# A quarter of 21 products moved from VectorE to ScalarE and GpSimd, in an induced attention with a gated feed-forward layer

## The chip, the core and the metric

The kernel runs on one core of one Trainium2 chip. A core has five engines that run side by side and wait for each other by semaphores: TensorE (PE; its weight loads are shown as PEld), VectorE (DVE), ScalarE (ACT), GpSimd (POOL) and SyncE (SP, here a queue for DMAs). Each engine takes its own instructions strictly in the order in which the program gives them. Matmul results land in PSUM, which has 8 banks of 512 f32 columns; GpSimd cannot read PSUM, so what it is to work on must first be copied to SBUF. The metric is the time of one execution in microseconds of device time.

## The reference

An input of 4 batches of 12,416 rows of 128 channels goes through an induced set attention: 32 inducing vectors attend to the rows of a batch, and the rows attend to the result. What comes out, 49,664 rows, goes through a feed-forward layer with a sigmoid gate.

```
def mab(q, kv):
    s = scale * (q @ kv.transpose(0, 2, 1))
    s = s - s.max(-1, keepdims=True)
    a = np.exp(s)
    a /= a.sum(-1, keepdims=True) + 1e-09
    return a @ kv
h = mab(I, x)                 # I: the 32 inducing vectors, for each batch
y = mab(x, h)                 # 4 x 12416 x 128

gate = 1.0 / (1.0 + np.exp(-(y @ w_gate)))     # w_gate, w_val: 128 x 1536
val = y @ w_val
out = gate * val @ w_out                       # w_out: 1536 x 128
```

## The kernel before

The attention part is called stage 1 (inducing vectors over rows) and stage 2 (rows over the 32 vectors h). Stage 2 is never finished into y: the kernel folds h into the weights (`hw`, 32 rows in place of 128), so that both hidden matmuls of the feed-forward layer take the normalised attention weights `a2` (32 rows) as their input. Four such matmuls of 32 rows can be placed beside each other on TensorE; here the two of the value part and the two of the gate.

The feed-forward part is the frame of the whole program. Rows are taken in *blocks* of 512 (4 chunks of 128). The hidden width of 1536 is 12 slices of 128. For each block there are eight *steps*, alternately of two slices (`cnt=2`, 1024 columns) and of one (`cnt=1`, 512 columns). A pair of steps is called a slot here (one of 1024 and one of 512). Each batch has 24 blocks, 192 steps, 96 slots. For step t:

- `hidden_mm(st, "v")` fills the value's PSUM tile `v_ps` and, in `gate_fill(t + 2)`, the gate's `g_ps` of two steps later. The two-slice tiles have a double bank each (`v2`, `g2`), the one-slice tiles a bank each (`v1`, `g1`), and each tile exists once: v of step t can be filled only when the product of step t − 2 is done, g of step t + 2 only when the gate of step t is done. One bank (`acc`) gathers the output, one (`m`) serves stage 1 and 2.
- `gate(t)` on ScalarE writes t = tanh(g / 2) to SBUF as f16 (L1053).
- `product(t)` on VectorE makes u = (t + 1) · v, f16, in one instruction (L1071). The factor one half is applied at the very end.
- `project` issues the output matmuls (L1106), four per slice, with u as weights, one per chunk, and gathers 12 slices in `acc`. After a block's last slice ScalarE scales the bank into `o32` (L1124) and SyncE stores it.

In the main loop, step t issues `product(t)`, then `gate(t + 2)`, then what the plan puts beside this slot (all of stage 1 and 2 for later rows, cut in pieces by `plan_...` functions and hung on slots by number), and on odd steps `project` with room for 3 slices (4 when more than 3 are waiting). So the order on every engine is written out by this loop; no scheduler changes it. For products of two slices from step 4 on, the kernel replaces the wait for the gate by a hand-made one for the gate's fill of t + 2, which itself comes after the gate.

From the last third of the fourth batch on (`T0`) the gates are made ahead slice by slice, and all products are of two slices. A product of two slices there reads its gate from a ring in `xn`; this part is the same before and after.

Of the kernel before, what the change touches and what calls it, by code (L numbers as in the profile page):

```python
# [17 lines left out]
P = 128  # L18
GC = 16
BC = 4  # L20
# [6 lines left out]
def kernel(  # L27
# [90 lines left out]
    def keep_on(n, tag, src=idle):  # L118
        w_ps = ps.tile([P, 4, P], F32, tag=tag, name="w_ps")
        for _ in range(n):  # L120
            nc.tensor.matmul(w_ps[:], src[:, 0, :], src, start=True, stop=True)
# [11 lines left out]
        out=identf[:],  # L133
        in_=identf[:],
# [13 lines left out]
    wo16 = const.tile([P, NJ, C], F16, tag="wo16")  # L148
# [648 lines left out]
    for p in range(-2, NS - 3):  # L797
# [40 lines left out]
    c0, n = groups[sc]  # L838
# [3 lines left out]
    for j0, tag, copy in ((GC // 2, "v2", nc.scalar.copy), (GC - BC, "g1", nc.vector.tensor_copy)):  # L842
# [35 lines left out]
    for g in range(4):  # L878
# [4 lines left out]
            start=False,  # L883
            stop=True,
            skip_group_check=True,
# [12 lines left out]
        out=e32l[:], in0=e32[:], scalar1=lsum[:], scalar2=TINY, op0=ALU.mult, op1=ALU.add  # L898
# [16 lines left out]
    def h_add(k, first=False, last=False):  # L915
# [15 lines left out]
        out=nmx_a[:], in_=s2_a[:, 0:BC, :], axis=AX.X, op=ALU.max, negate=True  # L931
# [11 lines left out]
    for hf, tag in enumerate(("g1", "v1")):  # L943
# [41 lines left out]
    steps = []  # L985
    blocks = []
    first_step = {}
# [11 lines left out]
    T0 = first_step[(B - 1, 0)] + 2 * 16  # L999
    assert gates[T0]["j0"] == 0  # L1000
    steps = gates[:T0]
    singles = []
    for i in range(gates[T0]["block"], len(blocks)):
        for j in range(0, NJ, 2):
            steps.append(dict(block=i, j0=j, cnt=2, bank="vw" if j % 4 else "v2"))
        singles += [dict(block=i, j0=j, cnt=1, bank=f"gw{j % 3}") for j in range(NJ)]
    NST = len(steps)

    def hidden_mm(st, what, halves=False):
        tag = st.get("bank") or f"{what}{st['cnt']}"  # L1010
        pt = ps.tile([P, st["cnt"], 512], F32, tag=tag, name=f"{what}_ps")
        pieces, col = [], 0
        for b, c, nb in blocks[st["block"]]:
            pieces += [(k, b, c, nb, col) for k in range(st["cnt"])]
            col += nb * P
        if not halves and st["block"] < len(blocks) - 1:
            pieces.sort(key=lambda p: p[0])
        for k, b, c, nb, col in pieces:
            j = st["j0"] + k
            r = 32 * (j % 2 + (2 if what == "v" else 0))  # L1020
            a2r, o = a2[(b, c)]
            st[what + "end"] = nc.tensor.matmul(  # L1022
                pt[:, k, col : col + nb * P],
                hw[b][r : r + 32, j // 2, :],
                a2r[r : r + 32, o : o + nb, :].rearrange("p j t -> p (j t)"),
                start=True,
                stop=True,
            )
        st[what] = pt

    def gate_fill(t):
        if t < T0 + 2:
            hidden_mm(gates[t], "g", t == 0)

    def ring_t(i, n):
        c = i % 24 * BC
        return xn[B - 2][:, c : c + n * BC, :].rearrange("p (j a) c -> p j (a c)", a=BC)

    def single_fill(i):
        if i < len(singles):  # L1040
            hidden_mm(singles[i], "g")
# [5 lines left out]
    def gate(t):  # L1047
        if t < T0 + 2:
# [3 lines left out]
            for c, e in zip(cuts, cuts[1:]):  # L1052
                st["tanh"] = nc.scalar.activation(  # L1053
                    out=st["t"][:, :, c:e], in_=st["g"][:, :, c:e], func=AF.Tanh, scale=0.5
                )

    def product(t):
        st = steps[t]
        hidden_mm(st, "v")
        if t == 0:  # L1060
            keep_on(3, "acc")
        if t < T0:
            gate_fill(t + 2)
        else:
            single_fill(2 * (t - T0) + 3)
            single_fill(2 * (t - T0) + 4)
            st["t"] = ring_t(2 * (t - T0), 2)
        st["u"] = up.tile([P, st["cnt"], 512], F16, tag=f"u{st['cnt']}", name="u16")
        cuts = [0, 256, 512] if t == 0 else [0, 512] if t < NST - 1 else [0, 384, 512]
        for c, e in zip(cuts, cuts[1:]):  # L1070
            u = nc.vector.scalar_tensor_tensor(  # L1071
                out=st["u"][:, :, c:e],
                in0=st["t"][:, :, c:e],
                scalar=1.0,
                in1=st["v"][:, :, c:e],
                op0=ALU.add,
                op1=ALU.mult,
            )
# [12 lines left out]

    def project(upto, now, room):
        while queue and queue[-1][0] < upto and room > 0:
            t, k = queue.pop()
            st = steps[t]
            j = st["j0"] + k
            if j == 0:
                acc[0] = ps.tile([P, BC, C], F32, tag="acc", name="acc_ps")
            todo = [(k, i) for i in range(BC)]
            if t == NST - 1:  # L1100
                k, _ = queue.pop()[1], None
                j = st["j0"] + k
                todo = [(n, i) for n in range(2) for i in range(BC - 1)] + [(n, BC - 1) for n in range(2)]
            for n, i in todo:
                e = st["j0"] + n
                nc.tensor.matmul(  # L1106
                    acc[0][:, i, :],
                    st["u"][:, n, ts(i, P)],
                    wo16[:, NI * (e % 2) + e // 2, :],
                    start=(e == 0 and i == 0),  # L1110
                    stop=(e == NJ - 1),
                    skip_group_check=True,
                )
            room -= 1
            if t == NST - 1:
                o32 = op.tile([P, BC, C], F32, tag="o32")
                nc.scalar.mul(out=o32[:, 0:2], in_=acc[0][:, 0:2], mul=0.5)
# [3 lines left out]
            elif j == NJ - 1:  # L1121
                block = blocks[st["block"]]
                o32 = op.tile([P, BC, C], F32, tag="o32")
                nc.scalar.mul(out=o32[:], in_=acc[0][:], mul=0.5)  # L1124
# [8 lines left out]
    for b in range(B):  # L1133
# [6 lines left out]
        for s in range(3 if b == 0 else 2, NG - 1):  # L1140
            k = o + 16 * s - 28
# [76 lines left out]
    for t in range(T0):  # L1218
        product(t)
        gate(t + 2)  # L1220
        if t % 2 == 0:
            beside(t // 2, False)
        else:
            beside(t // 2, True)
            project(t - 1, t, 3 if waiting(t - 1) <= 3 else 4)
    narrow.close()
    ps.open(ctx, "psw", "vw", "gw0", "gw1", "gw2")
    for t in range(T0, NST):
        product(t)
        six, part = divmod(t - T0, 3)  # L1230
        single_gate(2 * (t - T0) + 3)
        for i in range(2):
            if not project(t - 1, t, 1) and waiting(t - 1) >= 2:
                project(t - 1, t, 1)
# [36 lines left out]
```

## Time and profile before

| | |
|---|---|
| median of 3 runs | 713.96 us (713.81 to 714.0) |
| span of the profiled execution | 712.4 us |
| VectorE busy | 694.2 us (97%) |
| ScalarE busy | 678.6 us (95%) |
| TensorE busy | 649.5 us (91%) |
| GpSimd busy | 449.2 us (63%) |
| granted TensorE clock, mean | 0.998 |

The span runs from the first to the last instruction of one profiled execution; the time of a run holds some 1.6 us more. In the lists, a row gives line, engine, operation, output and inputs, shapes and the number of instances, then the busy time in all and the mean of one in ns, and behind the second bar the idle time of the engine just before these instructions with what ended it. In the list by time a row is a run of like instructions on one engine: its start, how long it lasts from its first start to its last end, and their number. Instructions on an engine overlap a little: the next one starts before the last one's end, so a step from start to start is shorter than the duration.

### The profile page before, as it was taken

To read this page: it belongs to the slowest core of one execution; us is meant where nothing else is said; L and a number is where in the kernel's file an instruction comes from. 1 tells how busy PE (TensorE), PEld (TensorE's weight loads), DVE (VectorE), ACT (ScalarE), POOL (GpSimd) and SP (SyncE) were. 2 spreads that over 40 slices of the span, in tenths; PEclk is the share of its full clock that TensorE was granted. 3 is DMA by queue.
4 is the path that set the end of the run, shared out by engine and by line. 5 is a ranking of instruction groups with operands and counts; after the bars stand their busy time and mean duration, and the time that the engine had idled before them with its cause. 6 is when DMAs were issued, how large, how long until landed. Compare 5 with 4: busy or idle time off the path is not lost.

```text
span 712.4 us, 21620 instructions
## 1 busy us (share of the span) xinstructions
PE 649.5 (91%) x8475; PEld 394.2 (55%) x8475; DVE 694.2 (97%) x806; ACT 678.6 (95%) x1103; POOL 449.2 (63%) x785
## 2 busy tenths in 40 slices
PE   7999899998999999999998989999899999899996
PEld 4555455555555555655555655555555555555555
DVE  4799999999999999999999999999999999999997
ACT  4799999999999999999999999999999999999996
POOL 4568865877558978668657887587748356372300
PEclk9999999999999999999999999999999999999999
DMA  8979964263693174155485142221222131221201
GB/s 171 176 136 174 149 129 103 76 120 81 118 159 81 57 126 103 56 120 114 92 149 112 53 76 67 55 76 38 70 76 61 46 60 60 61 61 46 71 37 46
DMA packets 117110, 65.23 MB, mean 92 GB/s; under 512 B 100208, under 2 KB 101392, under 8 KB 117008
## 3 DMA queue, kind: packets, MB, share of 16 engines
q1 hardware_dynamic: 112320, 49.83, 31.4%
q0 software_dynamic: 4416, 13.90, 11.1%
q8 instruction: 66, 1.08, 0.6%
q14 instruction: 36, 0.29, 0.1%
q10 hardware_dynamic: 272, 0.13, 0.1%
HBM read 27.80 MB, written 25.43 MB: 75 GB/s over the span
## 4 chain that ended last, share of the span: by engine, by line
DVE 38%; PE 30%; issue 15%; ACT 14%; DMA 2%; DVEq 1%; POOL 0%; ACTq 0%; POOLq 0%
DVE u L1071 36%; PE acc_ps L1106 14%; PE v_ps L1022 11%; ACT t L1053 11%; PE g_ps L1022 2%; DMA xn<-in_x_dram 2%; ACT o L1124 2%; ACT xn L1045 1%; PE hp_ps L296 1%; DVE nm L248 1%; DVEq L1071 0%; POOL xn L95 0%; ACT a1T L261 0%; ACT e L662 0%; ACT hwt L483 0%
## 5 line engine op out<-in xcount | busy, mean ns | idle before, releaser
L1071 DVE SCALAR_TENSOR_TENSOR u<-t,v_ps 128x512 f16<-128x512 f16 x609 | 528.8, 947 | 1.0 <-ACT t L1053 0.5
L1053 ACT ACTIVATE t<-g_ps 128x512 f16<-128x512 f32 x609 | 464.5, 821 | 11.0 <-ACT t L1053 4.3
L1106 PE MATMUL acc_ps<-wo,u 128*128 128x128 f16 x4656 | 334.5, 220 | 3.2 <-ACT o L1124 0.8
L1106 PEld LDWEIGHTS <-u 128*128 128x128 f16 x4656 | 262.7, 98 | 112.9 <-issue 109.4
L1022 PE MATMUL v_ps<-a2r,hwt 32*128 32x512 f16 (+1 forms) x1188 | 278.6, 372 | 47.1 <-DVE u L1071 43.5
L1022 PE MATMUL g_ps<-a2r,hwt 32*128 32x512 f16 (+1 forms) x1188 | 293.6, 376 | 0.5 <-DVE u L1071 0.2
L1022 PEld LDWEIGHTS <-hwt 32*128 32x128 f16 x2424 | 92.0, 91 | 156.7 <-issue 104.3
L1071 DVE SCALAR_TENSOR_TENSOR u<-xn,v_ps 128x1024 f16<-128x1024 f16 (+1 forms) x127 | 142.9, 1206 | 0.3 <-PE g_ps L1022 0.3
L1045 ACT ACTIVATE xn<-g_ps 128x512 f16<-128x512 f32 x249 | 129.0, 606 | 1.9 <-PE g_ps L1022 0.6
L692 POOL TENSOR_TENSOR a2n<-e,rs 128x2048 f16<-128x2048 f16 (+3 forms) x25 | 86.8, 3475 | 5.0 <-DVE rs L681 2.1
L670 POOL TENSOR_TENSOR sum<-e 128x256 f32<-128x256 f16 (+1 forms) x23 | 15.4, 672 | 117.0 <-ACT e L662 117.0
L453 POOL TENSOR_TENSOR near<-sme,minus 128x16 f32<-128x16 f32 (+1 forms) x22 | 65.2, 2964 | 1.6
L1124 ACT ACTIVATE o<-acc_ps 128x512 f32<-128x512 f32 x96 | 58.0, 604 | 0.0
L647 POOL TENSOR_SCALAR rise<-rise 128x256 f32<-128x256 f32 (+6 forms) x110 | 30.3, 275 | 9.6
L650 POOL TENSOR_TENSOR top<-top,rise 128x128 f32<-128x128 f32 (+3 forms) x88 | 28.5, 323 | 7.3
L670 POOL TENSOR_TENSOR sum<-sum 128x128 f32<-128x128 f32 (+3 forms) x92 | 28.4, 309 | 7.2
L646 POOL TENSOR_TENSOR rise<-top 128x128 f32<-128x128 f32 (+3 forms) x88 | 27.3, 311 | 6.9
L646 POOL TENSOR_TENSOR rise<-sc 128x256 f32<-128x256 f32 (+1 forms) x18 | 13.3, 736 | 21.2 <-ACT sc L636 21.1
L653 POOL TENSOR_TENSOR sc<-sc,top 128x512 f32<-128x512 f32 (+1 forms) x18 | 19.5, 1086 | 1.4
L602 PEld LDWEIGHTS <-xT 128*128 128x128 f16 x388 | 13.1, 96 | 11.7 <-issue 11.3
L95 POOL DMA_DIRECT2D xn<-in_x_dram x25 | 15.0, 607 | 6.5 <-DMA xn<-in_x_dram 5.6
L602 PE MATMUL s_ps<-hT,xT 128*128 128x32 f16 x388 | 18.1, 178 | 0.1
(161 smaller groups left out, 321.7 us busy)
## 6 DMA issues: line engine op xcount, KB each, us to landing
out_dram<-o SPq DMA_DIRECT2D x96, 256.0 KB, 2.1
xn<-in_x_dram POOLq DMA_DIRECT2D x19, 512.0 KB, 7.2
xn<-in_x_dram POOLq DMA_DIRECT2D x4, 544.0 KB, 6.0
a2r<-a2n SPq DMA_TRANSPOSE x29, 4.4
xT<-xn SPq DMA_TRANSPOSE x27, 4.4
xn<-in_x_dram POOLq DMA_DIRECT2D x1, 384.0 KB, 14.9
wg<-in_moe_w_gate_dram POOLq DMA_DIRECT2D x1, 384.0 KB, 16.4
wv<-in_moe_w_val_dram POOLq DMA_DIRECT2D x1, 384.0 KB, 16.4
```

Source lines behind the costliest of these rows:

```text
L453: nc.gpsimd.tensor_tensor(out=near, in0=x, in1=minus, op=ALU.pow)
L602: nc.tensor.matmul(s2[:, j, :], xT[b][:, c + j, :], hT16[b][:], start=(j == 0), stop=whole and j == j1 - 1, skip_group_check=True,)
L646: nc.gpsimd.tensor_tensor(out=r, in0=far, in1=near, op=ALU.subtract)
L647: nc.gpsimd.tensor_scalar(out=r, in0=r, scalar1=BIG, scalar2=0.0, op0=ALU.min, op1=ALU.max)
L670: nc.gpsimd.tensor_tensor(out=d[:, 0:n, :], in0=src[:, :, 0:w], in1=src[:, :, w : 2 * w], op=ALU.add)
L692: eng.tensor_tensor(out=a2n[:, 0:n, :, :], in0=e.unsqueeze(2).to_broadcast((P, n, 4, m)), in1=rs.unsqueeze(2).unsqueeze(3).to_broadcast((P ...
L1022: st[what + "end"] = nc.tensor.matmul(pt[:, k, col : col + nb * P], hw[b][r : r + 32, j // 2, :], a2r[r : r + 32, o : o + nb, :].rearrange ...
L1045: nc.scalar.activation(out=ring_t(i, 1), in_=singles[i]["g"][:], func=AF.Tanh, scale=0.5)
L1053: st["tanh"] = nc.scalar.activation(out=st["t"][:, :, c:e], in_=st["g"][:, :, c:e], func=AF.Tanh, scale=0.5)
L1071: u = nc.vector.scalar_tensor_tensor(out=st["u"][:, :, c:e], in0=st["t"][:, :, c:e], scalar=1.0, in1=st["v"][:, :, c:e], op0=ALU.add, op1= ...
L1106: nc.tensor.matmul(acc[0][:, i, :], st["u"][:, n, ts(i, P)], wo16[:, NI * (e % 2) + e // 2, :], start=(e == 0 and i == 0), stop=(e == NJ - 1),
L1124: nc.scalar.mul(out=o32[:], in_=acc[0][:], mul=0.5)
```

## The change

In each of the first three batches seven slots (k = 5, 33, 49, 65, 77, 85, 93; in all of them the step of two slices is the block's second, slices 3 and 4) are put in the set `aside`. There:

- ScalarE copies the last 256 of the 1024 columns of `v_ps` to SBUF as f32 (`far`). The copy is issued behind the fill of v and ahead of `gate(t + 2)`.
- VectorE makes the first 768 columns of u in one instruction.
- GpSimd makes the last 256 columns in two: mid = far · t, u = mid + far.
- The output matmuls for these 256 columns (slice 4, chunks 2 and 3) go behind all others of their block.

The queue of output matmuls is now in single matmuls in place of slices, with room for 14 per call, and 9 just after an aside step. The buffers of u are 6 for two slices, as before, and 4 for one. For the products of steps t + 2, t + 4 and t + 6 behind an aside step t the hand-made wait is left out, so that they wait for fill and gate as the framework finds it.

```diff
+    aside = set()
+    for b in range(B - 1):
+        for k in (5, 33, 49, 65, 77, 85, 93):
+            aside.add(first_step[(b, 0)] + 2 * k)
+    after = {t + d for t in aside for d in (2, 4, 6)}
...
+    def aside_take(t):
+        st = steps[t]
+        st["far"] = tp.tile([P, 256], F32, tag="far", name="far", bufs=2)
+        nc.scalar.copy(out=st["far"], in_=st["v"][:, 1, 256:512])
+
+    def aside_product(t):
+        st = steps[t]
+        mid = tp.tile([P, 256], F32, tag="mid", name="mid", bufs=1)
+        nc.gpsimd.tensor_tensor(out=mid, in0=st["far"], in1=st["t"][:, 1, 256:512], op=ALU.mult)
+        nc.gpsimd.tensor_tensor(out=st["u"][:, 1, 256:512], in0=mid, in1=st["far"], op=ALU.add)
...
     def product(t):
         st = steps[t]
         hidden_mm(st, "v")
...
+        if t in aside:
+            aside_take(t)
-        st["u"] = up.tile([P, st["cnt"], 512], F16, tag=f"u{st['cnt']}", name="u16")
+        st["u"] = up.tile(
+            [P, st["cnt"], 512], F16, tag=f"u{st['cnt']}", name="u16", bufs=6 if st["cnt"] == 2 else 4
+        )
...
+        if t in aside:
+            nc.vector.scalar_tensor_tensor(
+                out=flat(st["u"][:])[:, 0:768],
+                in0=flat(st["t"][:])[:, 0:768],
+                scalar=1.0,
+                in1=flat(st["v"][:])[:, 0:768],
+                op0=ALU.add,
+                op1=ALU.mult,
+            )
+            aside_product(t)
+            return
...
-        if st["cnt"] == 2 and 4 <= t < T0:
+        if st["cnt"] == 2 and 4 <= t < T0 and t not in after:
...
-    queue = [(t, k) for t in range(NST) for k in range(steps[t]["cnt"])]
+    queue = [(t, k, i) for t in range(NST) for k in range(steps[t]["cnt"]) for i in range(BC)]
+    for t in aside:
+        end = max(k for k in range(NST) if steps[k]["block"] == steps[t]["block"])
+        for i in (2, 3):
+            queue.remove((t, 1, i))
+            queue.insert(queue.index((end, steps[end]["cnt"] - 1, BC - 1)) + 1, (t, 1, i))
...
-            project(t - 1, t, 3 if waiting(t - 1) <= 3 else 4)
+            project(t - 1, t, 9 if t - 1 in aside else 14)
```

How this stands on ScalarE around step 154 (k = 77 of the first batch). Before: gates (t), the output copy o of the block before, gates. In brackets are the semaphores that an instruction waits for, named by the engine that raises them.

```order
L1053 ACTIVATE t_3717<-g_ps 128x1024 [waits DVE_49,PE_49,Activation_49]
L1053 ACTIVATE t_3725<-g_ps 128x512 [waits DVE_49,PE_49]
L1124 ACTIVATE o_3739<-acc_ps 128x512 [waits DMAHW4_49,PE_49]
L1053 ACTIVATE t_3750<-g_ps 128x1024 [waits DVE_49,PE_49,Activation_49]
L1053 ACTIVATE t_3758<-g_ps 128x512 [waits DVE_49,PE_49]
```

And of the change, the same stretch:

```order
L1058 ACTIVATE t_3737<-g_ps 128x1024 [waits DVE_49,PE_49,Activation_49]
L1058 ACTIVATE t_3745<-g_ps 128x512 [waits DVE_49,PE_49]
L1160 ACTIVATE o_3759<-acc_ps 128x512 [waits DMAHW4_49,PE_49]
L1065 COPY far<-v_ps 128x256 [waits PE_49]
L1058 ACTIVATE t_3775<-g_ps 128x1024 [waits DVE_49,PE_49,Activation_49]
L1058 ACTIVATE t_3783<-g_ps 128x512 [waits DVE_49,PE_49]
```

The copy far stands between the output copy and the gate of step 156.

On VectorE the products around the same step were, the third of these being that of step 154:

```order
L1071 SCALAR_TENSOR_TENSOR u_3715<-t_3687,v_ps 128x1024 [waits DVE_49,PE_49]
L1071 SCALAR_TENSOR_TENSOR u_3723<-t_3695,v_ps 128x512 [waits PE_49,Activation_49]
L1071 SCALAR_TENSOR_TENSOR u_3748<-t_3717,v_ps 128x1024 [waits DVE_49,PE_49]
L1071 SCALAR_TENSOR_TENSOR u_3756<-t_3725,v_ps 128x512 [waits PE_49,Activation_49]
L1071 SCALAR_TENSOR_TENSOR u_3779<-t_3750,v_ps 128x1024 [waits DVE_49,PE_49]
L1071 SCALAR_TENSOR_TENSOR u_3787<-t_3758,v_ps 128x512 [waits PE_49,Activation_49]
```

and are now:

```order
L1105 SCALAR_TENSOR_TENSOR u_3735<-t_3707,v_ps 128x1024 [waits PE_49]
L1105 SCALAR_TENSOR_TENSOR u_3743<-t_3715,v_ps 128x512 [waits PE_49,Activation_49]
L1094 SCALAR_TENSOR_TENSOR u_3770<-t_3737,v_ps 128x768 [waits Activation_49]
L1105 SCALAR_TENSOR_TENSOR u_3781<-t_3745,v_ps 128x512 [waits PE_49]
L1105 SCALAR_TENSOR_TENSOR u_3801<-t_3775,v_ps 128x1024 [waits PE_49,Activation_49]
L1105 SCALAR_TENSOR_TENSOR u_3809<-t_3783,v_ps 128x512 [waits PE_49,Activation_49]
```

The product of step 154 is of 768 columns and waits for ScalarE where it waited for TensorE; that of step 156 waits for both.

On GpSimd the two new operations stand between the last steps of a row maximum (L653) and the row sums (L670) of stage 2:

```order
L653 TENSOR_TENSOR sc<-sc,top 128x512 [waits Pool_49]
L1070 TENSOR_TENSOR mid<-far,t_3737 128x256 [waits Activation_49]
L1071 TENSOR_TENSOR u_3770<-mid,far 128x256 [waits DVE_49,PE_49,Pool_49]
L670 TENSOR_TENSOR sum_3838<-e 128x256 [waits Activation_49]
L670 TENSOR_TENSOR sum_3840<-sum_3838 128x128 [waits Pool_49]
```

Before, L670 followed L653 directly.

More of the change, by code (lines that the diff above doesn't have):

```diff
@@ L1055, in gate, with flat @@
                 )
+    def aside_take(t):
[7 more added lines that the diff above has]
+        nc.gpsimd.tensor_tensor(out=st["u"][:, 1, 256:512], in0=mid, in1=st["far"], op=ALU.add)
+    def flat(x):
+        return x.rearrange("p k c -> p (k c)")
     def product(t):
@@ L1088 @@
     acc = [None]
-    queue = [(t, k) for t in range(NST) for k in range(steps[t]["cnt"])]
+    queue = [(t, k, i) for t in range(NST) for k in range(steps[t]["cnt"]) for i in range(BC)]
[4 more added lines that the diff above has]
+            queue.insert(queue.index((end, steps[end]["cnt"] - 1, BC - 1)) + 1, (t, 1, i))
+    last = queue[-2 * BC :]
+    queue[-2 * BC :] = sorted(last, key=lambda e: (e[2] == BC - 1, e[1], e[2]))
+    ends = {steps[e[0]]["block"]: e for e in queue}
     queue.reverse()
@@ L1093, in project @@
         while queue and queue[-1][0] < upto and room > 0:
-            t, k = queue.pop()
+            t, k, i = e = queue.pop()
             st = steps[t]
             j = st["j0"] + k
-            if j == 0:
+            if j == 0 and i == 0:
                 acc[0] = ps.tile([P, BC, C], F32, tag="acc", name="acc_ps")
-            todo = [(k, i) for i in range(BC)]
-            if t == NST - 1:
[L1101 to L1116, printed above, removed]
+            nc.tensor.matmul(
+                acc[0][:, i, :],
+                st["u"][:, k, ts(i, P)],
+                wo16[:, NI * (j % 2) + j // 2, :],
+                start=(j == 0 and i == 0),
+                stop=(j == NJ - 1),
+                skip_group_check=True,
+            )
+            room -= 1
+            if ends[st["block"]] != e:
+                continue
+            o32 = op.tile([P, BC, C], F32, tag="o32")
+            if t == NST - 1:
                 nc.scalar.mul(out=o32[:, 0:2], in_=acc[0][:, 0:2], mul=0.5)
@@ L1120, in project @@
                 nc.sync.dma_start(ov0[:, 0, 2:4, :], o32[:, 2:4])
-            elif j == NJ - 1:
+            else:
                 block = blocks[st["block"]]
-                o32 = op.tile([P, BC, C], F32, tag="o32")
                 nc.scalar.mul(out=o32[:], in_=acc[0][:], mul=0.5)
@@ L1232 @@
         for i in range(2):
-            if not project(t - 1, t, 1) and waiting(t - 1) >= 2:
-                project(t - 1, t, 1)
+            if not project(t - 1, t, BC) and waiting(t - 1) >= 2 * BC:
+                project(t - 1, t, BC)
             if i == 0:
```

## The prediction

> **What bounds the kernel now.** I read the page first, then the groups by shape, then a table by stage, then the order of time inside one slot.
>
> ```profile
> span 712.4 us, 21620 instructions
> PE 649.5 (91%) x8475; PEld 394.2 (55%) x8475; DVE 694.2 (97%) x806; ACT 678.6 (95%) x1103; POOL 449.2 (63%) x785
> L1071 DVE SCALAR_TENSOR_TENSOR u<-t,v_ps 128x1024 f16<-128x1024 f16 x303 | 368.4, 1216 | 0.2
> L1071 DVE SCALAR_TENSOR_TENSOR u<-xn,v_ps 128x768 f16<-128x768 f16 x1 | 0.9, 948 | 0.0
> 200.00:300.00 100.00, 92.77 (x1296) 56.59 (x1294) 100.00 (x118) 98.40 (x152) 77.49 (x131) 1.00 0.45 97
> 300.00:400.00 100.00, 91.70 (x1153) 55.33 (x1151) 100.00 (x117) 97.95 (x148) 71.10 (x120) 1.00 0.54 110
> PE v_ps L1022 <- DVE u L1071: 43.5, 212, 0.8
> ```
>
> The two rows of the table by stage (busy PE, PEld, DVE, ACT, POOL) say it best: VectorE is busy for all of 100.00 us in each, ScalarE for 98, TensorE for 92. The products at L1071 lose 0.2 us over 303 instances. So VectorE sets the pace, and anything that holds it up, or relieves it, moves the end by as much. But the others have little to give: TensorE waits for VectorE 43.5 us in all, about 0.2 us at a time.
>
> Now one slot in order of time; it is step 154, one of the 21 that the change touches (k = 77 of the first batch). Its product starts at 168.08.
>
> ```profile
> 165.75 1.81 DVE L1071 SCALAR_TENSOR_TENSOR u<-t,v_ps 128x512 f16<-128x512 f16 x2
> 166.35 1.81 DVE L1071 SCALAR_TENSOR_TENSOR u<-t,v_ps 128x1024 f16<-128x1024 f16 x2
> 167.48 1.81 DVE L1071 SCALAR_TENSOR_TENSOR u<-t,v_ps 128x512 f16<-128x512 f16 x2
> 166.38 1.51 ACT L1053 ACTIVATE t<-g_ps 128x1024 f16<-128x1024 f32 x2 [0.16 <-ACT t L1053]
> 167.62 0.39 PE L1022 MATMUL v_ps<-a2r,hwt 32*128 32x512 f16 x2
> 167.63 0.39 PE L1022 MATMUL g_ps<-a2r,hwt 32*128 32x512 f16 x2
> 167.78 0.60 ACT L1124 ACTIVATE o<-acc_ps 128x512 f32<-128x512 f32 x1
> 168.26 1.53 ACT L1053 ACTIVATE t<-g_ps 128x1024 f16<-128x1024 f32 x2
> ```
>
> The three VectorE rows are overlapping pairs of products, so their starts give the pace: a 512-wide product takes its successor's place after 0.60 (165.75 to 166.35), a 1024-wide one after 1.13 (166.35 to 167.48), a slot of both 1.73. The next 1024-wide product therefore starts at 167.48 + 0.60 = 168.08. Its operand v_ps is in one double bank, free only when the last 1024-wide product ends (166.35 + 1.22 = 167.57); the fill runs from 167.62 to 168.01 with the gate's beside it to 168.02. So the fill is ready 0.06 before it is used. That is the whole margin of this kernel. ScalarE comes to its two gates at 166.38, after a gap of 0.16 us, and from there works without a pause: gates, the output copy o at 167.78, the next gate at 168.26.
>
> **The change, part by part.**
>
> *Saved on VectorE.* The 1024-wide product takes 1216 ns, the 768-wide one that the program already has 948: 0.267 us less, and 21 of them make −5.6 us. All of it would be gain, as VectorE has no idle time here.
>
> *The copy, and who waits for it.* In the order, the shortened product no longer waits for TensorE, although it reads v_ps, which TensorE has just filled; it waits for ScalarE alone (in some slots also for an old GpSimd write). Of ScalarE's instructions only the copy of v_ps into far comes after that fill. So the product waits for the end of the copy. Its first 512 columns lie in one bank, its last 256 in the bank that the copy reads.
>
> And the copy has its turn after the output copy o. All 21 slots are the second pair of a block, and there the previous block's o stands directly ahead of it, as in the order shown above. In the trace o starts at 167.78 and what is next on ScalarE at 168.26. The new copy takes that place (v_ps has been full since 168.01). Its length is between these:
>
> ```profile
> L311 ACT COPY hst<-hp_ps 128x129 f32<-128x129 f32 x8 | 2.3, 293 | 0.0
> L1117 ACT ACTIVATE o<-acc_ps 128x256 f32<-128x256 f32 x1 | 0.4, 384 | 2.5 <-PE acc_ps L1106 2.5
> L483 ACT CAST hwt<-hw_ps 128x384 f16<-128x384 f32 x8 | 3.8, 482 | 0.0
> 463.73 0.39 PE L1022 MATMUL g_ps<-a2r,hwt 32*128 32x512 f16 x2
> 464.15 1.22 DVE L1071 SCALAR_TENSOR_TENSOR u<-t,v_ps 128x1024 f16<-128x1024 f16 x1
> ```
>
> I take the row of its own width, 0.38 us; 0.29 and 0.48 are the bounds. What a wait costs beyond the releaser's end is read where VectorE is late: a fill ends at 463.73 + 0.39 = 464.12 and the product starts at 464.15, some 0.04 later. So the product starts at 168.26 + 0.38 + 0.04 = 168.68 in place of 168.08: VectorE stands for 0.60 us to save 0.27. Over 21 slots the stall is +12.6 us (10.7 to 14.7 by the bounds). Behind the waiting product stands VectorE's whole queue, and for its end waits the fill of the same double bank two steps on; nothing catches up, since no later slot has spare time on VectorE. ScalarE itself is no further loss: the copy's turn of about 0.27 us (0.60 long rows follow each other after 0.48, so a 0.38 one after about 0.27) is less than the 0.33 by which VectorE falls back in the same slot.
>
> The trace has no place where both engines read one bank. The Trainium skill, "PSUM — Partial Sum Buffer", section "PSUM bank collisions raise a hardware error", says that two engines may not access the same bank at once in the same partitions, two reads included and whichever columns they touch, and that a scheduler has to order them. By that rule the quarter that was cut off cannot be copied beside the product and the wait must be there; no run here shows it, and without it the sum would be that of the first rival below.
>
> *The second wait instruction.* In 8 of the 21 slots the product waits for ScalarE by an instruction of its own ahead of it; and the three 1024-wide products after each aside slot (steps +2, +4, +6), which lose their hand-made wait for the gate's fill, now wait for TensorE by such an instruction and for ScalarE by themselves.
>
> ```profile
> L1071 DVEq EVENT_SEMAPHORE  x734: 21/21/1312, 30.0 to 705.1; - x184
> ```
>
> One lasts 21 ns when it waits for nothing. Standing last before a product that is 0.06 from being late, of which the hand-over takes 0.04, it can cost nothing (0.02 of margin hides it) or about 0.06 (its own 0.02 and a second hand-over of 0.04). I take the middle, 0.03, for 63 products: +1.9 us (0 to 3.8), and 0.05 for the 8, which have no margin: +0.4.
>
> *TensorE's order.* The output matmuls are as many as before. With the new room the projections of the slots around an aside hold 9, 13, 12 and 14 in place of 12 each.
>
> ```profile
> 168.54 0.84 PE L1106 MATMUL acc_ps<-wo,u 128*128 128x128 f16 x12
> 169.35 0.39 PE L1022 MATMUL v_ps<-a2r,hwt 32*128 32x512 f16 x2
> ```
>
> Twelve take 0.84 and one lasts 0.22, so one more is 0.056. The fill at 169.35 comes as the last one ends; VectorE's product before it ended at 168.08 + 1.22 = 169.30. Two more matmuls (0.11) thus may delay that fill by nothing up to 0.11; one more is inside the margin. I take 0.04 for 21 slots: +0.8 us (0 to 2.3). The 9 saves nothing, as that fill waits for the late product.
>
> *GpSimd.* Two operations of 256 columns at about 0.73 each (L646 and L650 below) are 1.5 us.
>
> ```profile
> L650 POOL TENSOR_TENSOR top<-sc,rise 128x256 f32<-128x256 f32 x15 | 11.0, 731 | 1.2
> L646 POOL TENSOR_TENSOR rise<-sc 128x256 f32<-128x256 f32 x15 | 11.0, 730 | 18.2 <-ACT sc L636 18.2
> 169.04 1.08 POOL L653 TENSOR_TENSOR sc<-sc,top 128x512 f32<-128x512 f32 x1
> 171.95 0.67 POOL L670 TENSOR_TENSOR sum<-e 128x256 f32<-128x256 f16 x1 [1.83 <-ACT e L662]
> ```
>
> They stand behind L653, which ends at 170.12, and ahead of L670, which waits for ScalarE until 171.95: 1.83 us of idle time for 1.5. Their result is read only at the block's end, three to four slots of 1.73 us after the product. Cost nothing; without that gap it would be up to 1.5 us of delay on GpSimd, still ahead of the block's end.
>
> *Sum.* −5.6 + 12.6 + 1.9 + 0.4 + 0.8 = +10.1 us on the span of 712.4, that is 722.5. The median of the runs shown is 713.96, 1.6 above the span: **724 us**. By the low bounds +5.1 (719), by the high ones +15.6 (730).
>
> **The rivals.**
>
> *Faster: the product does not wait for the copy.* If what it awaits on ScalarE were only its gate, long done, the 5.6 us would be kept, less up to 2.7 for waits and matmul order: 708 to 711. For it speaks that the profile has VectorE as the bound and that ScalarE and GpSimd have room; against it that the order then would still need a wait for TensorE's fill, and names none. It decides as soon as the product starts within 0.3 us of its old place. 5%.
>
> *Less slow: the copy gets ahead.* If o were done earlier, the copy would start with the fill's end, 168.05, and the product at 168.47: 0.39 lost for 0.27, +2.6 us, with the small terms up to 5: 716.5 to 719. Against it: ScalarE runs from the late gate at 166.38 without a pause, and o is ahead in its queue. 5%.
>
> *Slower still: ScalarE falls behind.* It has 0.16 us of rest in a slot. If the copy's 0.27 and the extra copies and exponentials that follow some slots push the next gates past their products, some 0.15 to 0.3 us more go in each of 21: 727 to 730. Against it: VectorE falls back 0.33 in the same slot. 12%.
>
> *The same.* Stall and saving would have to cancel, a stall of 0.27 in place of 0.60, and the small terms be nothing. 3%.
>
> **How the numbers follow.** My forecast, a net loss of 0.33 us in each aside slot and 3 us of small terms, has 75%. The range is 719 to 729: below it lie the first two rivals and the same, above it little. A measurement of this kernel can tell about 0.2%, 1.4 us, from no change. Faster 0.05, the same 0.03, slower 0.92.
>
> **What would show it.** Idle time of VectorE before the 768-wide product, put down to the copy far on ScalarE, of about 0.6 us, 21 times (12 to 13 us in all, where 0.2 stood); o, the copy and the gate in an unbroken row on ScalarE; the 768-wide product at 948 ns; hundredths of a microsecond before the three 1024-wide products after it; no wait of TensorE for GpSimd's u. I am wrong if the 768-wide products start without idle time, or if TensorE or GpSimd ends the larger waits.

## The result, and the profile after

| | before | after |
|---|---|---|
| median of 4 runs | 713.98 us (713.81 to 714.04) | 724.87 us (724.80 to 724.94) |
| ratio, with its 95% interval | | 1.0149 (1.0136 to 1.0161) |
| span of the profiled execution | 712.4 us | 723.2 us |

The change makes the kernel 1.5% slower. 724 us had been forecast, in a range of 719 to 729.

The page after, its head, then the groups by shape on VectorE, then the table of who waited for whom (total, times, longest):

```profile
span 723.2 us, 21464 instructions
PE 649.4 (90%) x8475; PEld 395.8 (55%) x8475; DVE 694.0 (96%) x806; ACT 685.3 (95%) x1124; POOL 478.4 (66%) x827
```

```profile
L1105 DVE SCALAR_TENSOR_TENSOR u<-t,v_ps 128x1024 f16<-128x1024 f16 x282 | 343.3, 1217 | 0.1
L1094 DVE SCALAR_TENSOR_TENSOR u<-t,v_ps 128x768 f16<-128x768 f16 x21 | 20.1, 955 | 11.7 <-ACT far L1065 11.7
```

```profile
POOL mid L1070 <- ACT far L1065: 24.5, 10, 4.4
DVE u L1094 <- ACT far L1065: 11.7, 21, 0.6
```

VectorE now stands idle before every one of the 21 short products, 11.7 us in all, and what ends it is each time the copy far. No row of the table has TensorE waiting for GpSimd's part of u, and none has anything waiting for GpSimd's two operations but GpSimd itself, so its own wait for far holds nobody up.

The slot of step 154 by time, the lines that answer to those of before (VectorE, ScalarE, TensorE, GpSimd):

```profile
170.60 0.95 DVE L1094 SCALAR_TENSOR_TENSOR u<-t,v_ps 128x768 f16<-128x768 f16 x1 [0.52 <-ACT far L1065]
171.47 0.68 DVE L1105 SCALAR_TENSOR_TENSOR u<-t,v_ps 128x512 f16<-128x512 f16 x1
...
168.30 1.51 ACT L1058 ACTIVATE t<-g_ps 128x1024 f16<-128x1024 f32 x2 [0.16 <-ACT t L1058]
169.70 0.60 ACT L1160 ACTIVATE o<-acc_ps 128x512 f32<-128x512 f32 x1
170.18 0.39 ACT L1065 COPY far<-v_ps 128x256 f32<-128x256 f32 x1
170.43 2.72 ACT L1058 ACTIVATE t<-g_ps 128x1024 f16<-128x1024 f32 x3
...
169.53 0.39 PE L1027 MATMUL v_ps<-a2r,hwt 32*128 32x512 f16 x2
...
171.82 0.67 POOL L1070 TENSOR_TENSOR mid<-far,t 128x256 f32<-128x256 f32 x1
172.57 0.73 POOL L1071 TENSOR_TENSOR u<-mid,far 128x256 f16<-128x256 f32 x1
174.23 0.67 POOL L670 TENSOR_TENSOR sum<-e 128x256 f32<-128x256 f16 x1 [0.93 <-ACT e L662]
```

ScalarE goes gates, o, copy, gate without a pause. v_ps is full at 169.53 + 0.39 = 169.92; the copy runs from 170.18 to 170.57, and the product starts at 170.60. It would have started at 170.00 by the pace of before (168.08 − 166.35 = 1.73 after the last 1024-wide product; that one started at 168.27). That is the 0.60 us of the forecast. The row's 0.52 us of idle time is less, as it counts from the end of the product before (169.40 + 0.68 = 170.08), and products overlap by 0.08. GpSimd's two operations fit into the gap ahead of L670, of which 0.93 us remain.

To see every step, the start of each product in the profile after is taken against that of the same step before; what follows is by how much this lag grows from step to step, summed over the 21 slots (t is the aside step; the rows for t + 4 to t + 10 take in the narrow step just ahead).

| where the lag grows | us in all | per slot |
|---|---|---|
| product of step t (stall) | +13.4 | 0.60 to 0.61, in the first two slots 0.70 and 0.67; 0.67 in the 8 where the wait for ScalarE is an instruction of its own |
| step t + 1 (768 columns, not 1024) | −5.5 | −0.26 |
| t + 2, t + 4, t + 6 | +0.7, +0.8, +0.5 | 0.03 to 0.04 |
| t + 8, t + 10 (14 output matmuls) | +0.9, −0.2 | 0.03 |
| all other steps | +0.7 | 0.05 at 13 products of t + 16 |

### The profile page after: what moved, and what is told of

It reads as the page before. It is cut to its first block, busy times and chain, and to the rows that moved or that the text cites. A ratio compares the mean times of both kernels' runs of the same rounds, so it can differ in the third digit from the quotient of the medians.

```text
span 723.2 us, 21464 instructions
## 1 busy us (share of the span) xinstructions
PE 649.4 (90%) x8475; PEld 395.8 (55%) x8475; DVE 694.0 (96%) x806; ACT 685.3 (95%) x1124; POOL 478.4 (66%) x827
## 4 chain that ended last, share of the span: by engine, by line
DVE 38%; PE 26%; issue 16%; ACT 12%; POOL 5%; DMA 2%; DVEq 0%; ACTq 0%; POOLq 0%
DVE u L1105 34%; PE acc_ps L1141 12%; PE v_ps L1027 9%; ACT t L1058 7%; DVE u L1094 3%; PE g_ps L1027 2%; DMA xn<-in_x_dram 2%; ACT o L1160 2%; POOL a2n L692 2%; ACT xn L1050 1%; POOL near L453 1%; ACT far L1065 1%; POOL sum L670 1%; DVE nm L248 1%; PE hp_ps L296 1%
## 5 line engine op out<-in xcount | busy, mean ns | idle before, releaser
L1105 DVE SCALAR_TENSOR_TENSOR u<-t,v_ps 128x512 f16<-128x512 f16 (+1 forms) x588 | 510.2, 938 | 0.9 <-ACT t L1058 0.5
L1027 PEld LDWEIGHTS <-hwt 32*128 32x128 f16 x2424 | 93.7, 91 | 167.0 <-issue 114.4
L670 POOL TENSOR_TENSOR sum<-e 128x256 f32<-128x256 f16 (+1 forms) x23 | 15.5, 672 | 77.8 <-ACT e L662 77.8
L670 POOL TENSOR_TENSOR sum<-sum 128x128 f32<-128x128 f32 (+3 forms) x92 | 28.4, 309 | 7.2
L1070 POOL TENSOR_TENSOR mid<-far,t 128x256 f32<-128x256 f32 x21 | 14.1, 673 | 27.5 <-ACT far L1065 24.5
L1094 DVE SCALAR_TENSOR_TENSOR u<-t,v_ps 128x768 f16<-128x768 f16 x21 | 20.1, 955 | 11.7 <-ACT far L1065 11.7
L653 POOL TENSOR_TENSOR sc<-sc,top 128x512 f32<-128x512 f32 (+1 forms) x18 | 19.5, 1085 | 1.4
L602 PEld LDWEIGHTS <-xT 128*128 128x128 f16 x388 | 13.0, 96 | 11.7 <-issue 11.3
```

What stands on the lines that cost most here:

```text
L670: nc.gpsimd.tensor_tensor(out=d[:, 0:n, :], in0=src[:, :, 0:w], in1=src[:, :, w : 2 * w], op=ALU.add)
L1027: st[what + "end"] = nc.tensor.matmul(pt[:, k, col : col + nb * P], hw[b][r : r + 32, j // 2, :], a2r[r : r + 32, o : o + nb, :].rearrange ...
L1094: nc.vector.scalar_tensor_tensor(out=flat(st["u"][:])[:, 0:768], in0=flat(st["t"][:])[:, 0:768], scalar=1.0, in1=flat(st["v"][:])[:, 0:768 ...
L1105: u = nc.vector.scalar_tensor_tensor(out=st["u"][:, :, c:e], in0=st["t"][:, :, c:e], scalar=1.0, in1=st["v"][:, :, c:e], op0=ALU.add, op1= ...
```

## The experiments

All were timed in turn with the kernel before on the same chip; its median there was 713.97 (e1 to e4), 713.99 (e5 to e8) and 714.06 us (e9 to e11). The edits of e1 to e4 are against the changed kernel. The question behind them is whether the wait for the copy is all there is to it.

### e1: the hand-made waits kept

```diff
-    after = {t + d for t in aside for d in (2, 4, 6)}
+    after = set()
```

> The changed kernel, but the products of steps +2, +4, +6 after an aside step keep the hand-made wait for the gate's fill. Theory: the hundredths that stand before these 63 products (0.66 + 0.84 + 0.54 = 2.0 us in the profile of the changed kernel) come from the wait instruction of their own; without it 724.9 - 2.0 = 722.9 us. Rival 1: they come from TensorE's new order of the output matmuls (9, 13, 12, 14), which stays: 724.9. Rival 2: the hand-made wait holds them up, since the gate is late behind the copy: over 726.

Measured: 724.09 us, ratio to before 1.0143 (1.0123 to 1.0163). By the lags the growth at t + 2, t + 4 and t + 6 falls from +2.0 to +0.1 us, so it is the second wait instruction that makes the hundredths. But the growth at t + 8 rises from +0.9 to +1.6: where the product had been late anyway, part of the 14 matmuls' cost had been hidden. By the medians 0.8 of the 2.0 us are won, less than the theory had (722.9), and the intervals of the two ratios overlap, so that the size is rough. The wait instruction is shown as the cause of those hundredths; of what it costs, 0.7 us come back at t + 8.

### e2: the copy reads something else

```diff
-        nc.scalar.copy(out=st["far"], in_=st["v"][:, 1, 256:512])
+        nc.scalar.copy(out=st["far"], in_=st["t"][:, 1, 256:512])
```

> The changed kernel, but ScalarE's copy reads the gate's tile t in SBUF in place of v_ps, so that the 768-wide product has no copy to wait for; every engine does as many operations of the same sizes (the last quarter of the 21 products is computed from other data). Theory: the loss is the wait alone; 21 stalls of 0.64 (13.4 us) go, some 0.04 per slot for a wait instruction come in: 714.0 - 5.5 + 0.8 + 3.0 of small waits = 712.3 us. Rival: ScalarE's and GpSimd's new work is the loss (ScalarE falls behind): 718 to 725.

Measured: 721.81 us, 1.0105 (1.0089 to 1.0120). The theory falls here: the stall at step t does go, from 13.4 to 0.9 us, and 9.4 us come back two slots later, at t + 4. By time, the same slot (step 154; ScalarE, then TensorE, then VectorE):

```profile
169.90 0.60 ACT L1160 ACTIVATE o<-acc_ps 128x512 f32<-128x512 f32 x1
170.37 0.42 ACT L1065 CAST far<-t 128x256 f32<-128x256 f16 x1
170.67 3.04 ACT L1058 ACTIVATE t<-g_ps 128x1024 f16<-128x1024 f32 x4
...
171.26 0.39 PE L1027 MATMUL v_ps<-a2r,hwt 32*128 32x512 f16 x2
171.77 0.39 PE L1027 MATMUL g_ps<-a2r,hwt 32*128 32x512 f16 x2
171.83 0.37 PE L1027 MATMUL v_ps<-a2r,hwt 32*128 32x512 f16 x1
172.25 0.37 PE L1027 MATMUL g_ps<-a2r,hwt 32*128 32x512 f16 x1
172.56 0.90 PE L1141 MATMUL acc_ps<-wo,u 128*128 128x128 f16 x13
173.39 0.39 PE L1027 MATMUL v_ps<-a2r,hwt 32*128 32x512 f16 x2
...
173.89 1.22 DVE L1105 SCALAR_TENSOR_TENSOR u<-t,v_ps 128x1024 f16<-128x1024 f16 x1 [0.31 <-PE g_ps L1027]
```

In the slot of the kernel before that the prediction shows, v and g are filled within 0.01 us of each other (0.01 to 0.02 in 19 of the 21 slots, 0.07 and 0.11 in the first two). Here v of step 156 is filled at 171.26, but g of step 158 only at 171.77, since its bank comes free when the gate of step 156, behind the copy, is done (start 170.67 and 1.03 long). TensorE takes its queue in order: v and g of the next steps and 13 output matmuls follow, and the fill of v for step 158 comes at 173.39. The product for it starts 0.31 after VectorE had become free (its bracket names g, whose fill of the same moment ends less than 0.01 us after that of v). The measured time lies in the range of the rival (718 to 725), which had ScalarE fall behind. So ScalarE's gate, TensorE's fill of g and the matmuls behind it are a second limit, as near as VectorE.

### e3: the copy ahead of o

```diff
-                nc.scalar.mul(out=o32[:], in_=acc[0][:], mul=0.5)
-                b, c, nb = block[0]
-                nc.sync.dma_start(ov[b, :, c : c + BC, :], o32[:])
+                def put(...): ...          # the same two instructions
+                if now + 1 in aside:
+                    held.append(put)       # run in product(), right behind aside_take(t)
+                else:
+                    put()
```

> The changed kernel, but in the 21 slots ScalarE's copy stands ahead of the output copy o. Theory: of the 0.60 stall the part that is o's turn goes; the copy starts with the fill's end (0.04 after it) in place of 0.25 after it, so the product comes 0.20 earlier: 724.9 - 21 x 0.20 = 720.7 us. Rival: ScalarE now stands idle for some 0.25 us before the copy and falls behind, so that gates come late: no gain or a loss, 724 to 728.

Measured: 726.5 us, 1.0169 (1.0152 to 1.0186), above the changed kernel. The stall does fall as expected, from 13.4 to 8.3 us by the lags, but t + 2 and t + 4 grow from 1.5 to 8.0.

```profile
170.56 0.37 ACT L1066 COPY far<-v_ps 128x256 f32<-128x256 f32 x1 [0.15 <-PE g_ps L1028]
170.83 0.60 ACT L1166 ACTIVATE o<-acc_ps 128x512 f32<-128x512 f32 x1
171.32 2.58 ACT L1059 ACTIVATE t<-g_ps 128x1024 f16<-128x1024 f32 x3
```

ScalarE waits for the fill before the copy, o goes behind it, and the gate starts later still. This is the rival of the forecast for this run.

### e4: two products, one for each bank

```diff
-            nc.vector.scalar_tensor_tensor(out=flat(st["u"][:])[:, 0:768], ...)
+            for c, e in ((0, 512), (512, 768)):
+                u = nc.vector.scalar_tensor_tensor(out=flat(st["u"][:])[:, c:e], ...)
+                if c == 0:
+                    tc.declare_no_dep(u.ins, st["copy"].ins, reason="each reads a bank of its own")
+                    # and the hand-made wait for the gate's fill of t + 2
```

The hand-made waits are kept as in e1.

> The changed kernel with the 768-wide product as two, of 512 columns (the bank that the copy does not read, not waiting for it) and of 256 (waiting for it), and with the hand-made waits kept. Theory: only a shared bank needs the wait; the first product runs while the copy does, so of 1.13 us a slot 0.60 + 0.33 remain: 21 x -0.20 = -4.2, small waits and matmul order +2 to +3: 711.5 to 713 us, a little faster than before. Rival: the second instruction stalls as the one did, or VectorE and ScalarE hinder each other: 716 or more.

Measured: 721.44 us, 1.0098 (1.0083 to 1.0113). The first product does run while ScalarE copies from the tile's other bank, and the whole output is still computed; the stall at step t falls from 13.4 to 0.7 us and the two products keep 3.9 us. But 8.5 us come in at t + 2, where the product waits for g's fill, behind the late gate (step 154; ScalarE, TensorE, VectorE):

```profile
169.77 0.39 ACT L1065 COPY far<-v_ps 128x256 f32<-128x256 f32 x1
170.02 2.62 ACT L1058 ACTIVATE t<-g_ps 128x1024 f16<-128x1024 f32 x3
...
170.67 0.39 PE L1027 MATMUL v_ps<-a2r,hwt 32*128 32x512 f16 x2
171.14 0.39 PE L1027 MATMUL g_ps<-a2r,hwt 32*128 32x512 f16 x2
...
169.60 1.02 DVE L1095 SCALAR_TENSOR_TENSOR u<-t,v_ps 128x512 f16<-128x512 f16 x2
171.57 1.22 DVE L1112 SCALAR_TENSOR_TENSOR u<-t,v_ps 128x1024 f16<-128x1024 f16 x1 [0.35 <-PE g_ps L1027]
```

The first of the two products starts at 169.60, ahead of the copy (169.77 to 170.16), and runs on beside it. So what was expected of the bank is there, and the time is not; it is above the 716 of the rival, though the second product does not stall as the one did, and the first lasts 0.69 us beside the copy where the other products of 512 columns last 0.68.

### e5: the copy alone

The kernel before (products whole, no GpSimd, output matmuls in the order of before, all hand-made waits) and one copy of 256 columns from SBUF in each of the 21 slots, which nothing reads.

```diff
+        if t in aside:
+            aside_take(t)     # copies st["t"][:, 1, 256:512]
```

> The kernel before with one thing more: in the 21 slots ScalarE makes a copy of 256 columns of t in SBUF, behind o and ahead of the next gate, that nothing reads; products, GpSimd and the order of the output matmuls as before, the hand-made waits too. Theory (second limit): the gate behind the copy ends 0.27 later, it was done 0.07 before TensorE's fill of the gate two steps on, which thus is 0.2 late, and the product that waits for that fill too: 714.0 + 21 x 0.2 = 718.2 us. Rival: ScalarE has room for a copy (34 us of idle time in all): 714.0 to 714.5.

Measured: 719.77 us, 1.0081 (1.0066 to 1.0096).

```profile
169.12 0.42 ACT L1065 CAST far<-t 128x256 f32<-128x256 f16 x1
169.41 2.55 ACT L1058 ACTIVATE t<-g_ps 128x1024 f16<-128x1024 f32 x3
...
170.21 0.39 PE L1027 MATMUL v_ps<-a2r,hwt 32*128 32x512 f16 x2
170.51 0.39 PE L1027 MATMUL g_ps<-a2r,hwt 32*128 32x512 f16 x2
...
170.94 1.22 DVE L1094 SCALAR_TENSOR_TENSOR u<-t,v_ps 128x1024 f16<-128x1024 f16 x1 [0.18 <-PE g_ps L1027]
```

The gate behind the copy takes 1.03 from 169.41, g is filled at 170.51 where v is at 170.21, and the product at t + 2 is 0.27 late in each slot, 5.7 us in all: the copy's full turn (169.12 to 169.41 is 0.29). The forecast had 0.20 per slot, since it took 0.07 us between gate and g's fill for slack; in every one of the 21 slots 0.05 of it is still there in e5, so it is the hand-over. ScalarE has 34 us of idle time by the page and no room for a copy in these slots.

### e6 and e7: the short product alone, the order alone

e6 is the changed kernel without copy and GpSimd; e7 the kernel before with the output matmuls in the changed order.

```diff
 e6
-        if t in aside:
-            aside_take(t)
...
-            aside_product(t)
...
-                st["u"][:, k, ts(i, P)],
+                st["u"][:, 0 if t in aside and i > 1 else k, ts(i, P)],
 e7
-        if t in aside:        # no copy, no short product, after = set();
-            ...               # queue and room as changed
```

> The changed kernel without ScalarE's copy and without GpSimd's two operations; the 21 products have 768 columns and their last quarter isn't made (the output matmuls of that quarter read another part of the same product). Theory: the 0.26 per slot is not kept in full, since gate, gate's fill and TensorE's matmuls in their order bring the next fills no more than 0.1 to 0.2 us earlier, and the wait instructions cost some 2.5: 710.5 to 713 us. Rival: VectorE alone sets the pace, all is kept: 714.0 - 5.5 + 0.8 + 2.5 or less = 709 to 712 with no idle time of VectorE anywhere behind the short product.

> The kernel before with the output matmuls alone in the changed order (two of them last in the block, 9, 13, 12, 14 in place of 12 each); products whole, no copy, hand-made waits everywhere. Theory: only the 14 costs, 0.06 to 0.1 us of 21 times, 715.3 us (1.3 to 2 more than before). Rival: the order is free, 714.0; or the uneven calls cost every time, 717 or more.

Measured: e6 716.10 us, 1.0030 (1.0018 to 1.0041); e7 715.99 us, 1.0031 (1.0019 to 1.0042). The order alone costs 2.0 us, as forecast (1.3 to 2), most of it at t + 8 (+1.6 by the lags), where a call has 14 matmuls. The short product alone, with no operation added on ScalarE or GpSimd, is not faster than before: of the 5.5 us it saves by the lags nothing is left. 0.8 come in at t (its own wait instruction), 1.4 at t + 2, 3.3 at t + 4, 0.6 at t + 6 and 1.3 at t + 8. How much of the middle ones is wait instruction and how much a late fill isn't separated here; e9 leaves the wait instructions and the order out. It is slower than even the theory had (710.5 to 713), and far from the rival.

### e8: a slot without o

e4, one slot later, with the hand-made wait left out at t + 2 alone.

```diff
-            aside.add(first_step[(b, 0)] + 2 * k)
+            aside.add(first_step[(b, 0)] + 2 * k + 2)
...
+    after = {t + 2 for t in aside}
```

> The two-instruction form (512 columns not waiting for the copy, 256 waiting), but one slot later, where no output copy o is ahead of the copy on ScalarE; the hand-made wait is left out for step +2 alone. Theory: the gate behind the copy then ends before it is wanted, so nothing stands; of 0.20 saved per slot the late fills keep about half: 712.5 to 715 us, close to before. Rival: ScalarE has no room for the copy in any slot: 718 to 721, as with o ahead of it.

Measured: 720.07 us, 1.0089 (1.0074 to 1.0104). The two products save 4.1 us, the gate right behind the copy is in time (+1.0 at t + 2), but 6.6 us come in at t + 4: in 20 of the 21 slots an exponential of stage 2 (15 slots) or a copy sc (5) stands on ScalarE behind far and the two gates that follow it, and the next gate is behind all of these. The theory (712.5 to 715) is missed, and the time is in the rival's range (718 to 721). But the first slot, step 12, has neither o nor such an operation there, and in it the product at t + 2 loses nothing and that at t + 4 0.02 us of the 0.20 saved; the rest goes by t + 15, most of it at t + 6, t + 8 and t + 14 (0.04, 0.08 and 0.05). So the rival's "in any slot" isn't borne out; one slot is not a kernel, and no kernel with such slots alone was run.

### e9, e10, e11: what holds the gain of a short product back

All three make 21 products of 768 columns, with no copy and nothing on GpSimd (as e6, the last quarter isn't made), and the product of step t has the hand-made wait, which costs no instruction of its own.

```diff
 e9    output matmuls in the order of before, hand-made waits everywhere
 e10   as e9, but
+    after = {t + 2 for t in aside}
 e11   as e9, but the output matmuls in the changed order (9, 13, 12, 14), and in project():
+                n = BC // 2 if now + 1 in aside else BC
+                nc.scalar.mul(out=o32[:, 0:n], in_=acc[0][:, 0:n], mul=0.5)
```

> The short product alone without any of the small costs: 21 products of 768 columns (the last quarter not made; its output matmuls read another part of the same product), no copy, nothing on GpSimd, the output matmuls in the order of before (12 each), the hand-made wait at every product. Theory: the gate behind o ends at the same time as before and TensorE's fill of the gate two steps on comes right behind it, so the next product, which waits for that fill, starts only 0.03 earlier, not 0.26: 714.0 - 21 x 0.03 = 713.4 us. Rival: VectorE alone sets the pace and the small costs ate the gain: 714.0 - 5.5 = 708.5 us.

> As the short product alone with the order of before, but the product at step +2 doesn't wait for the gate's fill by hand. Theory: TensorE's 12 output matmuls and the fill behind them then bring it about 0.1 earlier at most, and part of that goes on its own wait instruction (0.04): 712.5 to 714 us. Rival (the hand-made wait alone holds the gain back): 709 to 710.5.

> The short product alone with hand-made waits everywhere, the changed order of the output matmuls (9, 13, 12, 14), and ScalarE relieved in these slots: the output copy o ahead makes half of its columns (half of 21 blocks' output isn't made or stored). Theory: with 0.24 off ScalarE and 9 matmuls the gate's and the value's fill come 0.2 earlier, so that most of the short product's gain reaches step +2, 21 x -0.2 = -4.2, and the order costs its 2.0: 711.5 to 712.5 us, below the short product with a full o. Rival: ScalarE isn't what holds the gain back: as the short product in the changed order, 714.5 to 716.

Measured: e9 713.91 us, 1.0003 (0.9993 to 1.0013); e10 714.71 us, 1.0010 (1.0001 to 1.0020); e11 712.19 us, 0.9975 (0.9966 to 0.9984). e9 came out 0.5 us above its theory (713.4) and far from its rival, e11 by its theory, e10 above both its theory and its rival. In e9 the step after the short product is earlier by 5.6 us in all, and 5.2 of them are given back at t + 2. Here is where, in the slot of step 154 of e9 (ScalarE, TensorE, VectorE):

```profile
168.15 3.08 ACT L1058 ACTIVATE t<-g_ps 128x1024 f16<-128x1024 f32 x4
...
168.43 0.84 PE L1137 MATMUL acc_ps<-wo,u 128*128 128x128 f16 x12
169.21 0.39 PE L1027 MATMUL v_ps<-a2r,hwt 32*128 32x512 f16 x2
169.24 0.39 PE L1027 MATMUL g_ps<-a2r,hwt 32*128 32x512 f16 x2
...
167.97 0.95 DVE L1092 SCALAR_TENSOR_TENSOR u<-t,v_ps 128x768 f16<-128x768 f16 x1
168.83 0.69 DVE L1106 SCALAR_TENSOR_TENSOR u<-t,v_ps 128x512 f16<-128x512 f16 x1
169.67 2.95 DVE L1106 SCALAR_TENSOR_TENSOR u<-t,v_ps 128x1024 f16<-128x1024 f16 x3 [0.15 <-PE g_ps L1027]
```

The short product ends at 168.92, so v could be filled from 168.97 on. It is filled at 169.21, at the end of the 12 output matmuls, and g at 169.24, at the end of the gate (168.15 + 1.03 = 169.18). Both are ready for the old pace and not before it. e10 takes the gate's fill out of the product's waits, and the product gains no more: in 18 of the 21 slots it gives back 0.02 to 0.05 us more than in e9, about the price of its own wait instruction, since the matmuls hold it too. e11 relieves both, ScalarE by half an o and TensorE by 3 matmuls in the right call (the same three engines, in the same slot):

```profile
167.07 0.39 ACT L1163 ACTIVATE o<-acc_ps 128x256 f32<-128x256 f32 x1
167.40 3.06 ACT L1058 ACTIVATE t<-g_ps 128x1024 f16<-128x1024 f32 x4
...
167.83 0.68 PE L1142 MATMUL acc_ps<-wo,u 128*128 128x128 f16 x9
168.44 0.39 PE L1027 MATMUL v_ps<-a2r,hwt 32*128 32x512 f16 x2
168.48 0.39 PE L1027 MATMUL g_ps<-a2r,hwt 32*128 32x512 f16 x2
...
167.36 0.95 DVE L1092 SCALAR_TENSOR_TENSOR u<-t,v_ps 128x768 f16<-128x768 f16 x1
```

The short product ends at 167.36 + 0.95 = 168.31, and the fills come 0.13 and 0.17 us behind it, where in e9 they came 0.29 and 0.32 us behind 168.92. By the lags 4.1 of the 5.6 us saved pass t + 2, and the changed order, by e7's price, takes 2.0 of them later on. The two reliefs weren't run one without the other under hand-made waits, so their shares are open. e11 is the only kernel here that is faster than before, by 0.25%, and it leaves out half of 21 blocks' output. No version that computes everything was found to beat the kernel before.

## Why the prediction was right, point by point

**The wait for the copy** was read from the order of the waits and priced from three rows. It measured 0.60 to 0.61 us in 11 of the 13 slots with a direct wait (0.60 forecast) and 0.67 in the 8 with their own instruction (0.65). The copy lasted 0.391 us where the row of 256 columns had 0.384. Summed, 13.4 us against 13.0.

**The saving on VectorE** measured 0.26 us per slot, 5.5 in all (5.6).

**The second wait instruction**: 2.0 us for the 63 products, forecast 1.9, and e1 shows that it is the cause. But 13 more products, 16 steps behind an aside step, have one too, at 0.05 each: they wait for GpSimd besides TensorE, and of what a product touches GpSimd has written only u. That makes 0.7 us that the forecast didn't have.

**TensorE's order**: +0.7 us net at t + 8 and t + 10, forecast 0.8; alone it costs 2.0 (e7), and 1.6 at t + 8 once the hand-made waits are kept (e1), as a late VectorE hides part of it. So this term and the one before share one margin, where the sum took them as two that add up, each inside bounds that began at nothing. That 2.7 us were forecast for both and 2.7 measured is partly luck.

**GpSimd**: nothing, as forecast; its operations took 0.673 and 0.726 us (0.73 each), and no TensorE wait names it.

The sum of the lags is 11.4 us, the span grew by 10.8, the median by 10.9; forecast were 10.1. (The lags run from the first product to the last; the stretches ahead of and behind them are together 0.6 us shorter than before.)

**What failed is a sentence that the sum didn't depend on, since behind the stall VectorE was the late one**: "VectorE sets the pace, and anything that holds it up, or relieves it, moves the end by as much", and with it "All of it would be gain, as VectorE has no idle time here". The first half held, the second did not. A VectorE that is busy for 100.00 of 100.00 us is at its limit, but ScalarE and TensorE were within hundredths of theirs in these slots (in e5 a copy's turn of 0.29 us makes the product 0.27 late; in e10 a product without the wait for the gate is no earlier), although they looked 2 and 8% idle. So the first rival was priced wrongly: without the wait, 708 to 711 us had been given, and e2 is 721.8. The second was wrong as well: with the copy ahead of o, 716.5 to 719 had been given, and e3 is 726.5, though e3 puts o behind the copy, where the rival had o done earlier; that wasn't run. And the reason for not counting ScalarE, that its turn of 0.27 is less than the 0.33 by which VectorE falls back, was right for the change but not beyond it: the stall itself hid the copy's second price, which e5 shows alone as 5.7 us (there for a copy whose turn is 0.29 us, where that of far is 0.25). That is the mechanism of the third rival, which the changed kernel doesn't show (+0.7 us at t + 2) and e2 to e5 do.

The Trainium skill, "Perfetto Trace Analysis", section "Identifying the Most-Contended Engine", has the engine of the highest occupancy as the one to improve first. In this case that engine is VectorE, and e9, which shortens 21 of its operations by 0.27 us at no cost to any other engine, measures 1.0003. By the rule of the Trainium skill, "PSUM — Partial Sum Buffer", section "PSUM bank collisions raise a hardware error", that two engines may not read one bank at once, the wait had to be there, and it stood in all 21 slots. In e4 the first product, which reads the bank that the copy does not, ran beside the copy: a product that leaves the copied bank alone need not wait. No run here has two engines read one bank at once.

## What to carry to other kernels

When work is moved from the busiest engine to two others, look in the very slot for what the new operation stands in front of on its engine, and follow that result for two or three slots: here the copy delayed a gate, the gate a fill, and in-order matmuls behind the fill the product. The busy shares did not tell how far the next limit was; the order of time in one slot could have, where the gate's fill came 0.01 us behind the value's, right behind the end of its gate. A short run that only removes the work, on the engine that is to be relieved, prices the most that a change can bring before anything is built around it.

## What the runs showed of the hardware that was not expected

- A wait instruction of its own directly before a product that is just in time costs 0.03 to 0.05 us (0.07 where the wait is for ScalarE's copy), although it lasts 0.021 us in the rows.
- A copy of 256 columns lasted 0.39 us on ScalarE from PSUM in f32 and 0.42 us from SBUF in f16; what came next started 0.25 us and 0.29 us after its start (changed kernel; e2, e5).
- The 768-wide product took 955 ns on average in the changed kernel, where GpSimd worked during each of the 21, and 955 ns in e6, where GpSimd's two operations are left out and in several slots nothing ran on it: GpSimd did not hold VectorE up.
